# Taking nine chunks of a gated product off VectorE: a ScalarE copy and two GpSimd operations in their place

## The chip, the cores and the metric

The kernel runs on one core of one Trainium2 chip. The metric is the device time of one execution in microseconds (us). The kernel before takes 713.96 us, the median of 3 runs (713.81 to 714.0).

## What is computed

Two things in a row, on x of 4 samples x 12416 tokens x 128 channels. First an attention block with 32 inducing points I: h = mab(I, x), then mab(x, h). Then a gated feed-forward layer of width 1536 on each token. Cut to its core:

```python
def mab(q, kv):                      # softmax attention with one head
    s = scale * (q @ kv.transpose(0, 2, 1))
    a = softmax(s)
    return a @ kv
y = mab(x, mab(I, x))                # (4, 12416, 128)
gate = 1.0 / (1.0 + np.exp(-(y @ w_gate)))
out = (gate * (y @ w_val)) @ w_out   # float32
```

## The kernel before

**Work and blocks.** The tokens of a sample are cut into blocks of 4 x 128 tokens. There are 97 blocks, 24 for each sample and one for the tokens left over. For a block the attention's second half and the two input products of the feed-forward layer are one matmul each: the normalised weights `a2r` (32 per token) times `hwt`, which holds h times the weights. The width of 1536 is 12 *chunks* of 128. A chunk of a block has 512 values in each of the 128 partitions, fp32 in PSUM, which is one bank.

For each chunk the engines do this:

- TensorE fills a bank with the gate's input (`g_ps`) and a bank with the value (`v_ps`), both at L1022 in `hidden_mm`.
- ScalarE takes tanh of half the gate's input from PSUM to fp16 (`t`, L1053, or `xn` at L1045 in the last stretch, where the results go to storage of x that is free by then).
- VectorE makes u = (tanh + 1) * value, from PSUM to fp16, at L1071 in `product`. The factor 0.5 of the sigmoid is left to the end.
- TensorE multiplies u with the chunk's part of w_out: four matmuls of 128 columns, added up over the 12 chunks in one bank, `acc_ps` (L1106 in `project`).
- After the 12th chunk ScalarE moves the bank out, times 0.5 (`o`, L1124), and SyncE stores it.

**The wide stretch.** For blocks 0 to 75 the chunks go in steps of two and one. From block 76 on (step number `T0`; the stretch of the change) no bank is needed for the attention any more, so PSUM is laid out anew: a block has six *steps* of two chunks, called steps 0 to 5 here. `v_ps` is one tile of two banks for a step, and there are two such tiles (tags "vw" and "v2") in turn, so the fill of a step waits until the product of two steps before is through. Three banks (`gw0` to `gw2`) hold gate inputs of single chunks, and one bank is `acc_ps`. VectorE makes one product of 1024 values in each step. ScalarE makes two single tanhs, each in an instruction of its own (`single_gate`).

**The order of the work.** It is written out by hand, and each engine goes through its own queue in order. In the wide stretch a step t is: the fill of v(t), the fills of two gate banks (the second chunk of step t+1 and the first of t+2), the product u(t), the tanh of step t+1's second chunk, then the output matmuls of step t-2's two chunks, one piece of what else is due, and the tanh of step t+2's first chunk. The output matmuls come out of a list of (step, chunk) pairs, `queue`. So the last chunks of a block are multiplied in step 1 of the block behind it, `o` comes there, and the first output matmul of the next block waits for `o`, since `acc_ps` is one bank.

**Other work in the stretch.** The weights `a2r` of the later blocks of the last sample are still made there: ScalarE does an exp (`e`, L662) for four blocks at a time, three times in the stretch (in step 0 of blocks 80, 84 and 89). Behind each GpSimd sums, inverts (L453) and spreads them (`a2n`, L692), and between these it subtracts maxima (L646 to L653).

**Waits.** They are put in from what each instruction reads and writes. Two engines that read the same PSUM tile are also put one behind the other, in the order of the program, unless the kernel says otherwise. It does so in two places, in these lines, of which the first stands at the start of the kernel for two engines that read two banks of a tile:

```python
tc.declare_no_dep(two.ins, one.ins, reason="each reads a bank of its own")
...
tc.declare_no_dep(u.ins, st["tanh"].ins, reason="the gate fill of t + 2 waits for it")
```

Of the kernel before, what the change touches and what calls it, by code (L numbers as in the profile page):

```python
# [9 lines left out]
F32 = mybir.dt.float32  # L10
# [3 lines left out]
ALU = mybir.AluOpType  # L14
# [3 lines left out]
P = 128  # L18
# [8 lines left out]
def kernel(  # L27
# [9 lines left out]
    nc = tc.nc  # L37
    B, N, C = x.shape
    m = inducing.shape[0]
    F = moe_w_gate.shape[1]  # L40
    NJ = F // P
# [19 lines left out]
    op = ctx.enter_context(tc.tile_pool(name="op", bufs=3))  # L61
# [23 lines left out]
    xn, xT = {}, {}  # L85
# [32 lines left out]
    def keep_on(n, tag, src=idle):  # L118
        w_ps = ps.tile([P, 4, P], F32, tag=tag, name="w_ps")
        for _ in range(n):  # L120
            nc.tensor.matmul(w_ps[:], src[:, 0, :], src, start=True, stop=True)
# [11 lines left out]
        out=identf[:],  # L133
        in_=identf[:],
# [662 lines left out]
    for p in range(-2, NS - 3):  # L797
# [13 lines left out]
        if p == EARLY - 2:  # L811
            we = const.tile([P, EARLY], F32, tag="we")
            nc.vector.tensor_reduce(
                out=nml[:, 0:1], in_=nm1[:, 0:EARLY], axis=AX.X, op=ALU.min
            )
            nc.scalar.activation(
                out=we[:], in_=nm1[:, 0:EARLY], func=AF.Exp, bias=nml[:, 0:1], scale=-1.0
# [20 lines left out]
    c0, n = groups[sc]  # L838
# [3 lines left out]
    for j0, tag, copy in ((GC // 2, "v2", nc.scalar.copy), (GC - BC, "g1", nc.vector.tensor_copy)):  # L842
# [26 lines left out]
        out=top[:],  # L869
        in_=mlT_ps.rearrange("o (g r) -> o r g", g=4),  # L870
        axis=AX.X,
        op=ALU.min,
# [5 lines left out]
    for g in range(4):  # L878
# [5 lines left out]
            stop=True,  # L884
# [13 lines left out]
        out=e32l[:], in0=e32[:], scalar1=lsum[:], scalar2=TINY, op0=ALU.mult, op1=ALU.add  # L898
# [5 lines left out]
        out=hw_parts[3],  # L904
        in0=hps[2],
        scalar=wl[:, 3:4],
        in1=hw_parts[2],
# [7 lines left out]
    def h_add(k, first=False, last=False):  # L915
# [15 lines left out]
        out=nmx_a[:], in_=s2_a[:, 0:BC, :], axis=AX.X, op=ALU.max, negate=True  # L931
# [3 lines left out]
        out=low[:],  # L935
        in0=s2_a[:, 0:BC, :],
        in1=nmx_a[:].unsqueeze(2).to_broadcast((P, BC, m)),
        op=ALU.add,
# [4 lines left out]
    for hf, tag in enumerate(("g1", "v1")):  # L943
# [10 lines left out]
        out=a2n_a[:],  # L954
        in0=e_a[:, :, 0:m],
        in1=rs_a.unsqueeze(2).to_broadcast((P, BC, m)),
        op=ALU.mult,
# [19 lines left out]
    def turn_b():  # L977
        rs_b = s2_inverse(nb, sme_b)
        a2n_b = s2_spread(BC, e_b[:, 0:BC, :], rs_b[:, 0:BC], nc.gpsimd)
        s2_turn_dma(0, NLO + BC, BC, a2n_b, "a2second")  # L980
        a2n_c = s2_spread(nb - BC, e_b[:, BC:nb, :], rs_b[:, BC:], nc.gpsimd)
        s2_turn_dma(0, NLO + 2 * BC, nb - BC, a2n_c, "a2r")


    steps = []
# [13 lines left out]
    T0 = first_step[(B - 1, 0)] + 2 * 16  # L999
    assert gates[T0]["j0"] == 0  # L1000
    steps = gates[:T0]
    singles = []
    for i in range(gates[T0]["block"], len(blocks)):
        for j in range(0, NJ, 2):
            steps.append(dict(block=i, j0=j, cnt=2, bank="vw" if j % 4 else "v2"))
        singles += [dict(block=i, j0=j, cnt=1, bank=f"gw{j % 3}") for j in range(NJ)]
    NST = len(steps)

    def hidden_mm(st, what, halves=False):
        tag = st.get("bank") or f"{what}{st['cnt']}"  # L1010
        pt = ps.tile([P, st["cnt"], 512], F32, tag=tag, name=f"{what}_ps")
        pieces, col = [], 0
        for b, c, nb in blocks[st["block"]]:
            pieces += [(k, b, c, nb, col) for k in range(st["cnt"])]
            col += nb * P
        if not halves and st["block"] < len(blocks) - 1:
            pieces.sort(key=lambda p: p[0])
        for k, b, c, nb, col in pieces:
            j = st["j0"] + k
            r = 32 * (j % 2 + (2 if what == "v" else 0))  # L1020
            a2r, o = a2[(b, c)]
            st[what + "end"] = nc.tensor.matmul(  # L1022
                pt[:, k, col : col + nb * P],
                hw[b][r : r + 32, j // 2, :],
                a2r[r : r + 32, o : o + nb, :].rearrange("p j t -> p (j t)"),
                start=True,
                stop=True,
            )
        st[what] = pt

    def gate_fill(t):
        if t < T0 + 2:
            hidden_mm(gates[t], "g", t == 0)

    def ring_t(i, n):
        c = i % 24 * BC
        return xn[B - 2][:, c : c + n * BC, :].rearrange("p (j a) c -> p j (a c)", a=BC)

    def single_fill(i):
        if i < len(singles):  # L1040
            hidden_mm(singles[i], "g")

    def single_gate(i):
        if i < len(singles):
            nc.scalar.activation(out=ring_t(i, 1), in_=singles[i]["g"][:], func=AF.Tanh, scale=0.5)  # L1045

    def gate(t):
        if t < T0 + 2:
# [3 lines left out]
            for c, e in zip(cuts, cuts[1:]):  # L1052
                st["tanh"] = nc.scalar.activation(  # L1053
                    out=st["t"][:, :, c:e], in_=st["g"][:, :, c:e], func=AF.Tanh, scale=0.5
                )

    def product(t):
        st = steps[t]
        hidden_mm(st, "v")
        if t == 0:  # L1060
            keep_on(3, "acc")
        if t < T0:
            gate_fill(t + 2)
        else:
            single_fill(2 * (t - T0) + 3)
            single_fill(2 * (t - T0) + 4)
            st["t"] = ring_t(2 * (t - T0), 2)
        st["u"] = up.tile([P, st["cnt"], 512], F16, tag=f"u{st['cnt']}", name="u16")
        cuts = [0, 256, 512] if t == 0 else [0, 512] if t < NST - 1 else [0, 384, 512]
        for c, e in zip(cuts, cuts[1:]):  # L1070
            u = nc.vector.scalar_tensor_tensor(  # L1071
                out=st["u"][:, :, c:e],
                in0=st["t"][:, :, c:e],
                scalar=1.0,
                in1=st["v"][:, :, c:e],
                op0=ALU.add,
                op1=ALU.mult,
            )
            if t == 0 and c == 0:
                turn_b()  # L1080
        if st["cnt"] == 2 and 4 <= t < T0:

            tc.declare_no_dep(u.ins, st["tanh"].ins, reason="the gate fill of t + 2 waits for it")
            tc.add_manual_dep(
                u.ins, gates[t + 2]["gend"].ins.name, AFTER, reason="tanh, gate fill, product"
            )

    acc = [None]
    queue = [(t, k) for t in range(NST) for k in range(steps[t]["cnt"])]
    queue.reverse()  # L1090

    def project(upto, now, room):
        while queue and queue[-1][0] < upto and room > 0:
            t, k = queue.pop()
            st = steps[t]
            j = st["j0"] + k
            if j == 0:
                acc[0] = ps.tile([P, BC, C], F32, tag="acc", name="acc_ps")
            todo = [(k, i) for i in range(BC)]
            if t == NST - 1:  # L1100
                k, _ = queue.pop()[1], None
                j = st["j0"] + k
                todo = [(n, i) for n in range(2) for i in range(BC - 1)] + [(n, BC - 1) for n in range(2)]
            for n, i in todo:
                e = st["j0"] + n
                nc.tensor.matmul(  # L1106
                    acc[0][:, i, :],
                    st["u"][:, n, ts(i, P)],
                    wo16[:, NI * (e % 2) + e // 2, :],
                    start=(e == 0 and i == 0),  # L1110
                    stop=(e == NJ - 1),
                    skip_group_check=True,
                )
            room -= 1
            if t == NST - 1:
                o32 = op.tile([P, BC, C], F32, tag="o32")
                nc.scalar.mul(out=o32[:, 0:2], in_=acc[0][:, 0:2], mul=0.5)
                nc.scalar.dma_start(ov0[:, 0, 0:2, :], o32[:, 0:2])
                nc.vector.tensor_scalar_mul(out=o32[:, 2:4], in0=acc[0][:, 2:4], scalar1=0.5)
                nc.sync.dma_start(ov0[:, 0, 2:4, :], o32[:, 2:4])  # L1120
            elif j == NJ - 1:
                block = blocks[st["block"]]
                o32 = op.tile([P, BC, C], F32, tag="o32")
                nc.scalar.mul(out=o32[:], in_=acc[0][:], mul=0.5)  # L1124
                b, c, nb = block[0]
                nc.sync.dma_start(ov[b, :, c : c + BC, :], o32[:])
                if now < NST:
                    return True
        return False
# [3 lines left out]
    for b in range(B):  # L1133
# [6 lines left out]
        for s in range(3 if b == 0 else 2, NG - 1):  # L1140
            k = o + 16 * s - 28
# [61 lines left out]
    def beside(slot, late):  # L1203
        for make in plan.pop((slot, late), ()):
            make()

    def waiting(upto):
        n = 0
        for e in reversed(queue):
            if e[0] >= upto:  # L1210
                break
            n += 1
        return n
# [13 lines left out]
    ps.open(ctx, "psw", "vw", "gw0", "gw1", "gw2")  # L1227
    for t in range(T0, NST):
        product(t)
        six, part = divmod(t - T0, 3)  # L1230
        single_gate(2 * (t - T0) + 3)
        for i in range(2):
            if not project(t - 1, t, 1) and waiting(t - 1) >= 2:
                project(t - 1, t, 1)
            if i == 0:
                for slot, late in ([(0, False), (0, True)], [(1, False)], [(1, True)])[part]:
                    beside(T0 // 2 + 2 * six + slot, late)
        single_gate(2 * (t - T0) + 4)
# [32 lines left out]
```

## Time and profile before

| what | value |
|---|---|
| time, median of 3 runs | 713.96 us (713.81 to 714.0) |
| span of the profiled execution | 712.4 us |
| instructions in it | 21620 |
| share of the span busy: TensorE, VectorE, ScalarE, GpSimd | 91%, 97%, 95%, 63% |
| mean granted TensorE clock | 0.998 |
| first and last tanh at L1045 | 565.3 and 705.2 us |
| chain that ended last: VectorE, TensorE, "issue", ScalarE | 38%, 30%, 15%, 14% |

How to read it: one execution was recorded on the chip. Its span goes from the first to the last instruction, and the execution has no time of its own beside that; the median of the runs is 1.6 us above the span, which is what lies around it. In the groups of instructions a row gives line, engine, operation, what is written from what, the shape and the count, then the busy time in us and the mean duration of one in ns, then idle time before it. In the timeline a row gives start and duration in us of instructions merged (xcount), and in brackets how long the engine was idle before and what released it. DVE is VectorE, ACT ScalarE, POOL GpSimd, PE TensorE. Instructions of one engine overlap in the records: the next one starts before the last one's result is written.

### The profile page before, as it was taken

The numbers are of one execution on the slowest core, as the hardware profiler recorded it, in microseconds if no ns is written. First come the engines' busy times: TensorE is split into PE (matmuls) and PEld (weight loads), VectorE is DVE, ScalarE is ACT, GpSimd is POOL, SyncE is SP. The second block draws the span as 40 slices with busy tenths as digits, with TensorE's granted clock in tenths as the row PEclk, the third lists the DMA queues.
The fourth block names the chain that finished last, engine by engine and source line by source line (L and its number), as shares of the span: only waits on it lengthen the run. The fifth ranks groups of instructions, "written<-read, shape, count | busy, mean of one in ns | idle before, by whom it ended". The sixth has DMA issues, their size and how long they took to land.

```text
span 712.4 us, 21620 instructions
## 1 busy us (share of the span) xinstructions
PE 649.5 (91%) x8475; PEld 394.2 (55%) x8475; DVE 694.2 (97%) x806; ACT 678.6 (95%) x1103; POOL 449.2 (63%) x785
## 2 busy tenths in 40 slices
PE   7999899998999999999998989999899999899996
PEld 4555455555555555655555655555555555555555
DVE  4799999999999999999999999999999999999997
ACT  4799999999999999999999999999999999999996
POOL 4568865877558978668657887587748356372300
PEclk9999999999999999999999999999999999999999
DMA  8979964263693174155485142221222131221201
GB/s 171 176 136 174 149 129 103 76 120 81 118 159 81 57 126 103 56 120 114 92 149 112 53 76 67 55 76 38 70 76 61 46 60 60 61 61 46 71 37 46
DMA packets 117110, 65.23 MB, mean 92 GB/s; under 512 B 100208, under 2 KB 101392, under 8 KB 117008
## 3 DMA queue, kind: packets, MB, share of 16 engines
q1 hardware_dynamic: 112320, 49.83, 31.4%
q0 software_dynamic: 4416, 13.90, 11.1%
q8 instruction: 66, 1.08, 0.6%
q14 instruction: 36, 0.29, 0.1%
q10 hardware_dynamic: 272, 0.13, 0.1%
HBM read 27.80 MB, written 25.43 MB: 75 GB/s over the span
## 4 chain that ended last, share of the span: by engine, by line
DVE 38%; PE 30%; issue 15%; ACT 14%; DMA 2%; DVEq 1%; POOL 0%; ACTq 0%; POOLq 0%
DVE u L1071 36%; PE acc_ps L1106 14%; PE v_ps L1022 11%; ACT t L1053 11%; PE g_ps L1022 2%; DMA xn<-in_x_dram 2%; ACT o L1124 2%; ACT xn L1045 1%; PE hp_ps L296 1%; DVE nm L248 1%; DVEq L1071 0%; POOL xn L95 0%; ACT a1T L261 0%; ACT e L662 0%; ACT hwt L483 0%
## 5 line engine op out<-in xcount | busy, mean ns | idle before, releaser
L1071 DVE SCALAR_TENSOR_TENSOR u<-t,v_ps 128x512 f16<-128x512 f16 x609 | 528.8, 947 | 1.0 <-ACT t L1053 0.5
L1053 ACT ACTIVATE t<-g_ps 128x512 f16<-128x512 f32 x609 | 464.5, 821 | 11.0 <-ACT t L1053 4.3
L1106 PE MATMUL acc_ps<-wo,u 128*128 128x128 f16 x4656 | 334.5, 220 | 3.2 <-ACT o L1124 0.8
L1106 PEld LDWEIGHTS <-u 128*128 128x128 f16 x4656 | 262.7, 98 | 112.9 <-issue 109.4
L1022 PE MATMUL v_ps<-a2r,hwt 32*128 32x512 f16 (+1 forms) x1188 | 278.6, 372 | 47.1 <-DVE u L1071 43.5
L1022 PE MATMUL g_ps<-a2r,hwt 32*128 32x512 f16 (+1 forms) x1188 | 293.6, 376 | 0.5 <-DVE u L1071 0.2
L1022 PEld LDWEIGHTS <-hwt 32*128 32x128 f16 x2424 | 92.0, 91 | 156.7 <-issue 104.3
L1071 DVE SCALAR_TENSOR_TENSOR u<-xn,v_ps 128x1024 f16<-128x1024 f16 (+1 forms) x127 | 142.9, 1206 | 0.3 <-PE g_ps L1022 0.3
L1045 ACT ACTIVATE xn<-g_ps 128x512 f16<-128x512 f32 x249 | 129.0, 606 | 1.9 <-PE g_ps L1022 0.6
L692 POOL TENSOR_TENSOR a2n<-e,rs 128x2048 f16<-128x2048 f16 (+3 forms) x25 | 86.8, 3475 | 5.0 <-DVE rs L681 2.1
L670 POOL TENSOR_TENSOR sum<-e 128x256 f32<-128x256 f16 (+1 forms) x23 | 15.4, 672 | 117.0 <-ACT e L662 117.0
L453 POOL TENSOR_TENSOR near<-sme,minus 128x16 f32<-128x16 f32 (+1 forms) x22 | 65.2, 2964 | 1.6
L1124 ACT ACTIVATE o<-acc_ps 128x512 f32<-128x512 f32 x96 | 58.0, 604 | 0.0
L647 POOL TENSOR_SCALAR rise<-rise 128x256 f32<-128x256 f32 (+6 forms) x110 | 30.3, 275 | 9.6
L650 POOL TENSOR_TENSOR top<-top,rise 128x128 f32<-128x128 f32 (+3 forms) x88 | 28.5, 323 | 7.3
L670 POOL TENSOR_TENSOR sum<-sum 128x128 f32<-128x128 f32 (+3 forms) x92 | 28.4, 309 | 7.2
L646 POOL TENSOR_TENSOR rise<-top 128x128 f32<-128x128 f32 (+3 forms) x88 | 27.3, 311 | 6.9
L646 POOL TENSOR_TENSOR rise<-sc 128x256 f32<-128x256 f32 (+1 forms) x18 | 13.3, 736 | 21.2 <-ACT sc L636 21.1
L653 POOL TENSOR_TENSOR sc<-sc,top 128x512 f32<-128x512 f32 (+1 forms) x18 | 19.5, 1086 | 1.4
L602 PEld LDWEIGHTS <-xT 128*128 128x128 f16 x388 | 13.1, 96 | 11.7 <-issue 11.3
L95 POOL DMA_DIRECT2D xn<-in_x_dram x25 | 15.0, 607 | 6.5 <-DMA xn<-in_x_dram 5.6
L602 PE MATMUL s_ps<-hT,xT 128*128 128x32 f16 x388 | 18.1, 178 | 0.1
(161 smaller groups left out, 321.7 us busy)
## 6 DMA issues: line engine op xcount, KB each, us to landing
out_dram<-o SPq DMA_DIRECT2D x96, 256.0 KB, 2.1
xn<-in_x_dram POOLq DMA_DIRECT2D x19, 512.0 KB, 7.2
xn<-in_x_dram POOLq DMA_DIRECT2D x4, 544.0 KB, 6.0
a2r<-a2n SPq DMA_TRANSPOSE x29, 4.4
xT<-xn SPq DMA_TRANSPOSE x27, 4.4
xn<-in_x_dram POOLq DMA_DIRECT2D x1, 384.0 KB, 14.9
wg<-in_moe_w_gate_dram POOLq DMA_DIRECT2D x1, 384.0 KB, 16.4
wv<-in_moe_w_val_dram POOLq DMA_DIRECT2D x1, 384.0 KB, 16.4
```

Of the source, the lines that this page charges most:

```text
L453: nc.gpsimd.tensor_tensor(out=near, in0=x, in1=minus, op=ALU.pow)
L602: nc.tensor.matmul(s2[:, j, :], xT[b][:, c + j, :], hT16[b][:], start=(j == 0), stop=whole and j == j1 - 1, skip_group_check=True,)
L646: nc.gpsimd.tensor_tensor(out=r, in0=far, in1=near, op=ALU.subtract)
L647: nc.gpsimd.tensor_scalar(out=r, in0=r, scalar1=BIG, scalar2=0.0, op0=ALU.min, op1=ALU.max)
L670: nc.gpsimd.tensor_tensor(out=d[:, 0:n, :], in0=src[:, :, 0:w], in1=src[:, :, w : 2 * w], op=ALU.add)
L692: eng.tensor_tensor(out=a2n[:, 0:n, :, :], in0=e.unsqueeze(2).to_broadcast((P, n, 4, m)), in1=rs.unsqueeze(2).unsqueeze(3).to_broadcast((P ...
L1022: st[what + "end"] = nc.tensor.matmul(pt[:, k, col : col + nb * P], hw[b][r : r + 32, j // 2, :], a2r[r : r + 32, o : o + nb, :].rearrange ...
L1045: nc.scalar.activation(out=ring_t(i, 1), in_=singles[i]["g"][:], func=AF.Tanh, scale=0.5)
L1053: st["tanh"] = nc.scalar.activation(out=st["t"][:, :, c:e], in_=st["g"][:, :, c:e], func=AF.Tanh, scale=0.5)
L1071: u = nc.vector.scalar_tensor_tensor(out=st["u"][:, :, c:e], in0=st["t"][:, :, c:e], scalar=1.0, in1=st["v"][:, :, c:e], op0=ALU.add, op1= ...
L1106: nc.tensor.matmul(acc[0][:, i, :], st["u"][:, n, ts(i, P)], wo16[:, NI * (e % 2) + e // 2, :], start=(e == 0 and i == 0), stop=(e == NJ - 1),
L1124: nc.scalar.mul(out=o32[:], in_=acc[0][:], mul=0.5)
```

## The change

In nine blocks of the wide stretch (77, 79, 81, 83, 86, 88, 91, 93 and 95) step 2 is split. VectorE's product at step 2 makes only the first of the two chunks. The second chunk goes another way. ScalarE copies its value from the second bank of `v_ps` to fp32 storage in SBUF (`aside_take`), in storage of x of the last sample, of which four pieces are used in turn. GpSimd multiplies this by the tanh and adds the value itself, which gives the same u = (tanh + 1) * value in fp16 (`aside_product`). The chunk's four output matmuls move from step 4 of the block to the end of the block's list, behind the 12th chunk, which is in step 1 of the next block. So in step 4 four output matmuls are left, and in step 1 of the next block there are twelve. `o` follows the moved chunk.

```diff
+    AWAY = 2
+    aside = {}
+    for i in (5, 7, 9, 11, 14, 16, 19, 21, 23):
+        t = T0 + (i * 4 - 16) * 3 // 2 + AWAY
+        assert steps[t]["j0"] == 2 * AWAY
+        aside[t] = len(aside)
...
+    def aside_take(t):
+        c = aside[t] % 4 * 24
+        spare = xn[B - 1][:, c : c + 24, :].rearrange("p j c -> p (j c)")
+        st = steps[t]
+        st["far"] = spare[:, 0:1024].bitcast(F32)
+        st["mid"] = spare[:, 1024:2048].bitcast(F32)
+        st["u1"] = spare[:, 2048:2560]
+        nc.scalar.copy(out=st["far"], in_=st["v"][:, 1, :])
+
+    def aside_product(t):
+        st = steps[t]
+        nc.gpsimd.tensor_tensor(out=st["mid"], in0=st["far"], in1=st["t"][:, 1, :], op=ALU.mult)
+        nc.gpsimd.tensor_tensor(out=st["u1"], in0=st["mid"], in1=st["far"], op=ALU.add)
...
+        n = 1 if t in aside else st["cnt"]
         for c, e in zip(cuts, cuts[1:]):
             u = nc.vector.scalar_tensor_tensor(
-                out=st["u"][:, :, c:e],
-                in0=st["t"][:, :, c:e],
+                out=st["u"][:, 0:n, c:e],
+                in0=st["t"][:, 0:n, c:e],
                 scalar=1.0,
-                in1=st["v"][:, :, c:e],
+                in1=st["v"][:, 0:n, c:e],
...
+    for t in aside:
+        end = max(k for k in range(NST) if steps[k]["block"] == steps[t]["block"])
+        queue.remove((t, 1))
+        queue.insert(queue.index((end, 1)) + 1, (t, 1))
+    ends = {steps[t]["block"]: (t, k) for t, k in queue}
...
-                    st["u"][:, n, ts(i, P)],
+                    st["u1"][:, ts(i, P)] if t in aside and n else st["u"][:, n, ts(i, P)],
...
-            elif j == NJ - 1:
+            elif ends[st["block"]] == (t, k):
...
         single_gate(2 * (t - T0) + 3)
+        if t in aside:
+            aside_take(t)
+            aside_product(t)
```

**ScalarE at block 81.** In the rows `xn` is the x storage that the tanhs go to (buffer 1758) or the copy goes to (buffer 5420); in brackets stand the engines and DMA queues whose counts the instruction waits for. Before, from the `o` of block 80 on:

```order
L1124 ACTIVATE o_12737<-acc_ps 128x512 [waits DMAHW3_49,PE_49]
L1045 ACTIVATE xn_1758<-g_ps 128x512 [waits DVE_49]
L1045 ACTIVATE xn_1758<-g_ps 128x512 [waits PE_49]
L1045 ACTIVATE xn_1758<-g_ps 128x512 [waits DVE_49,PE_49]
L1045 ACTIVATE xn_1758<-g_ps 128x512 [waits PE_49]
```

And the same place with the change, up to the `o` of block 81:

```order
L1150 ACTIVATE o_13119<-acc_ps 128x512 [waits DMAHW7_49,PE_49]
L1051 ACTIVATE xn_1758<-g_ps 128x512 [waits DVE_49]
L1051 ACTIVATE xn_1758<-g_ps 128x512 [waits PE_49]
L1070 COPY xn_5420<-v_ps 128x512 [waits DMASW1_49,DMASW0_49,DVE_49]
L1051 ACTIVATE xn_1758<-g_ps 128x512 [waits PE_49] x10
L1150 ACTIVATE o_13260<-acc_ps 128x512 [waits DMAHW0_49,PE_49]
```

The copy stands two tanhs behind the `o` of the block before, and ten tanhs wait behind it up to the block's own `o`. It waits for VectorE. In the built program the count that it waits for is that of the half product of its own step: in the first of the nine it waits for 687, while the value fills of that step and of the next one wait for 685 and 686, the products of the two steps before. The same holds for all nine.

**GpSimd at block 81.** `a2n` is the spread weights, `rise` the first of the chain of maxima for later blocks. Before:

```order
L692 TENSOR_TENSOR a2n<-e,rs 128x2048 [waits DMAHW1_49,Pool_49]
L646 TENSOR_TENSOR rise<-xT_3934 128x256
L647 TENSOR_SCALAR rise<-rise 128x256 [waits Pool_49]
L650 TENSOR_TENSOR top<-xT_3934,rise 128x256 [waits Pool_49]
L646 TENSOR_TENSOR rise<-top 128x16x8 [waits Pool_49]
```

With the change:

```order
L1074 TENSOR_TENSOR xn_5420<-xn_5420,xn_1758 128x512 [waits DMASW1_49,Activation_49]
L1075 TENSOR_TENSOR xn_5420<-xn_5420 128x512 [waits DMASW2_49,PE_49,Pool_49]
L646 TENSOR_TENSOR rise<-xT_3934 128x256
L647 TENSOR_SCALAR rise<-rise 128x256 [waits Pool_49]
L650 TENSOR_TENSOR top<-xT_3934,rise 128x256 [waits Pool_49]
```

The two operations of the aside chunk come between the spread and the maxima; the first of them waits for the copy.

More of the change, by code (lines that the diff above doesn't have):

```diff
@@ L1107, in project @@
                     acc[0][:, i, :],
-                    st["u"][:, n, ts(i, P)],
+                    st["u1"][:, ts(i, P)] if t in aside and n else st["u"][:, n, ts(i, P)],
                     wo16[:, NI * (e % 2) + e // 2, :],
                     start=(e == 0 and i == 0),
-                    stop=(e == NJ - 1),
+                    stop=(t == NST - 1 and e == NJ - 1) or ends[st["block"]] == (t, n),
                     skip_group_check=True,
```

## The prediction

> **What bounds the kernel now.** I read the page first, then the wide stretch by windows, then the groups by shape, and last the timeline of block 81 step by step, since in this kernel all engines are busy at once.
>
> ```profile
> span 712.4 us, 21620 instructions
> 571.97:706.60 134.63, 123.35 (x1502) 75.36 (x1499) 134.63 (x120) 132.43 (x260) 49.45 (x82) 1.00 0.21 57
> 594.60 46.47 DVE L1071 SCALAR_TENSOR_TENSOR u<-xn,v_ps 128x1024 f16<-128x1024 f16 x41
> ```
>
> The second row is the stretch from block 77 on. Its columns are TensorE, weight loads, VectorE, ScalarE, GpSimd. VectorE is busy for all of the 134.63 us, with 119 steps of one product each: 1.131 us a step. ScalarE is busy for 132.43 us, so hardly less. The third row, one piece of VectorE's timeline, has 41 products without a gap. So VectorE paces the stretch, and ScalarE is close behind. How close?
>
> ```profile
> 593.77 0.61 ACT L1124 ACTIVATE o<-acc_ps 128x512 f32<-128x512 f32 x1
> 594.25 2.58 ACT L1045 ACTIVATE xn<-g_ps 128x512 f16<-128x512 f32 x5
> 600.30 0.60 ACT L1124 ACTIVATE o<-acc_ps 128x512 f32<-128x512 f32 x1
> 607.03 0.60 ACT L1124 ACTIVATE o<-acc_ps 128x512 f32<-128x512 f32 x1
> ```
>
> With a backlog, five tanhs end 2.45 us after an `o` (596.83 against 594.38), 0.49 each. A block has 12 tanhs and one `o`: 13 x 0.49 = 6.37 us of the 6.79 (6 x 1.131). ScalarE has 0.42 us of slack in a block. VectorE off the bound is worth no more than ScalarE allows.
>
> **Part 1, VectorE: the gain.**
>
> ```profile
> L1071 DVE SCALAR_TENSOR_TENSOR u<-xn,v_ps 128x1024 f16<-128x1024 f16 x125 | 141.7, 1215 | 0.3 <-PE g_ps L1022 0.3
> L1071 DVE SCALAR_TENSOR_TENSOR u<-t,v_ps 128x512 f16<-128x512 f16 x306 | 208.1, 680 | 0.8 <-ACT t L1053 0.5 <-PE g_ps L1022 0.3
> L636 ACT COPY sc<-s_ps 128x512 f32<-128x512 f32 x18 | 10.7, 592 | 0.0
> L375 POOL TENSOR_TENSOR xT<-xT 128x512 f32<-128x512 f32 x7 | 8.9, 1272 | 3.6 <-ACT xT L358 3.5
> ```
>
> A product of 512 takes 0.68 us where one of 1024 takes 1.215, so each aside frees 0.535 us: 9 x 0.535 = 4.8 us at most.
>
> **Part 2, ScalarE: the copy and its wait.** A copy of this shape lasts 0.59 us like a tanh (0.60), so it takes a slot of 0.49. Nine of them are 4.4 us. Two blocks, one of them with a copy, then need 27 x 0.49 = 13.2 us of ScalarE, and VectorE needs 12 x 1.131 - 0.535 = 13.04: by sums alone ScalarE is the bound, and of the 0.535 some 0.34 would be left. But the copy also waits for the half product of its own step, as the order shows, and ten tanhs stand behind it. Block 81 before, where the products of steps 2, 3 and 4 start at 601.39, 602.52 and 603.65:
>
> ```profile
> 601.39 1.21 DVE L1071 SCALAR_TENSOR_TENSOR u<-xn,v_ps 128x1024 f16<-128x1024 f16 x1
> 602.52 2.35 DVE L1071 SCALAR_TENSOR_TENSOR u<-xn,v_ps 128x1024 f16<-128x1024 f16 x2
> 600.80 1.08 ACT L1045 ACTIVATE xn<-g_ps 128x512 f16<-128x512 f32 x2
> 600.80 2.06 ACT L1045 ACTIVATE xn<-g_ps 128x512 f16<-128x512 f32 x4
> 600.39 0.39 PE L1022 MATMUL v_ps<-a2r,hwt 32*128 32x512 f16 x2
> 600.96 0.61 PE L1106 MATMUL acc_ps<-wo,u 128*128 128x128 f16 x8 [0.17 <-ACT o L1124]
> 601.52 0.39 PE L1022 MATMUL v_ps<-a2r,hwt 32*128 32x512 f16 x2
> 604.78 1.22 DVE L1071 SCALAR_TENSOR_TENSOR u<-xn,v_ps 128x1024 f16<-128x1024 f16 x1
> 606.05 0.39 PE L1022 MATMUL v_ps<-a2r,hwt 32*128 32x512 f16 x2 [0.18 <-DVE u L1071]
> ```
>
> The second tanh starts at 601.28 (600.80 + 1.08 - 0.60), so ScalarE is free for the copy at 601.76, and v is in its bank since 600.78. The half product ends at 601.39 + 0.68 = 602.07. From the last two rows a wait across engines takes 0.05 (product ends 606.00, fill starts 606.05), so the copy starts at 602.12: 0.36 us of idle ScalarE. The two tanhs of step 4 then start at 602.61 and 603.10 instead of about 601.76 and 602.23. The second ends at 603.70, and the product of step 4 can start at 603.75. Without any wait the freed VectorE would be there at 603.12, and before it started at 603.65. So **VectorE waits 0.6 us at step 4, and the 0.535 is gone two steps after it was won**, with 0.1 us on top (0.09 by the unrounded starts). All nine copies stand at the same place behind an `o`, so I take 0.09 for each.
>
> **Part 3, the next block's `o`.** After that wait the tanhs have no lead over the products. Before, in block 81's step 4, the second tanh ended at 602.86, 0.79 before the product that reads it. How fast does it come back?
>
> ```profile
> 596.26 0.39 PE L1022 MATMUL v_ps<-a2r,hwt 32*128 32x512 f16 x2
> 597.24 0.39 PE L1022 MATMUL v_ps<-a2r,hwt 32*128 32x512 f16 x2
> 598.23 0.39 PE L1022 MATMUL v_ps<-a2r,hwt 32*128 32x512 f16 x2
> 604.92 0.39 PE L1022 MATMUL g_ps<-a2r,hwt 32*128 32x512 f16 x2
> 605.38 0.60 ACT L1045 ACTIVATE xn<-g_ps 128x512 f16<-128x512 f32 x1
> 607.04 1.22 DVE L1071 SCALAR_TENSOR_TENSOR u<-xn,v_ps 128x1024 f16<-128x1024 f16 x1
> L1106 PE MATMUL acc_ps<-wo,u 128*128 128x128 f16 x4656 | 334.5, 220 | 3.2 <-ACT o L1124 0.8 <-DVE u L1071 0.4
> ```
>
> When TensorE and ScalarE catch up after an exp, a step takes them 0.98 us, so 0.15 of lead a step. Three steps on, at step 1 of the next block, it is 0.45. Before, it was 1.0 there (the second tanh ends at 605.98, and the product that reads it, of block 82's step 1, starts at 607.04). So `o` comes 0.55 later against the products, and the four moved matmuls add up to 4 x 0.056 = 0.22 (eight of 0.22 each took 0.61 in a row, so they start 0.39 / 7 apart). From `o` to a product goes a fixed chain: `o` at 600.30, first output matmul 600.96, fill of step 3's value 601.52, and the product 0.46 later (the time from a fill's start at 604.92 to its reader's at 605.38): 601.98. It started at 602.52, so it had 0.54 of cover. An `o` that is 0.55 to 0.77 later costs 0 to 0.23 at step 3. ScalarE's next two tanhs free gate banks that TensorE fills before it goes on, which costs the like at step 4, and the value fill of step 0 is some 0.05 late for the same reason. Carrying these intervals forward step by step, I get 0.05 at step 0, 0.10 at step 3 and 0.15 at step 4: **0.3 us for each aside**; between 0, if the lead comes back sooner, and 0.5. Behind the asides of blocks 79, 83 and 88 an exp takes a further slot of 0.5 us in step 0, which makes 0.45 of it.
>
> **Part 4, what is hidden.** GpSimd's two operations take 2 x 1.27 = 2.5 us. Block 81 is the tightest, as GpSimd is in a spread there:
>
> ```profile
> 609.71 1.07 POOL L653 TENSOR_TENSOR xT<-xT,top 128x512 f32<-128x512 f32 x1
> 619.45 0.62 ACT L662 ACTIVATE e<-xT 128x512 f16<-128x512 f32 x1
> 599.54 3.61 POOL L692 TENSOR_TENSOR a2n<-e,rs 128x2048 f16<-128x2048 f16 x1
> 598.50:605.30 6.80, 6.41 (x77) 3.71 (x74) 6.80 (x7) 6.80 (x14) 6.22 (x9) 1.00 0.26 70
> ```
>
> The spread ends at 603.15, after the copy (602.72); the two end by 605.8. TensorE wants the chunk behind the 12th one, about 0.7 us into the fill of 606.05: a cover of 1.0 us, and in the other blocks more. Without it TensorE would stop for what is missing. The maxima behind them, which ended at 610.78, end 2.6 us later; the exp that reads them starts at 619.45, 6 us behind that. In the last row VectorE is busy for all 6.80 us with GpSimd busy for 6.22, so neither slows the other. [...] TensorE's matmuls are as many as before; the four taken out of step 4 free nothing, since it waits there for gate banks.
>
> **The sum.** Six asides: 0.09 + 0.3 = 0.39 each, 2.3 us. Three with an exp behind: 0.09 + 0.45 = 0.54 each, 1.6 us. Together +4.0 us: a span of 716.4 and, with the 1.6 us around it, **718.0 us**. With nothing for part 3 it is 9 x 0.09 = 0.8, so 714.8; with 0.5 for six and 0.65 for three it is 5.8, so 719.8.
>
> **The rivals.**
>
> *The lead holds (faster).* If the tanhs were far enough ahead when a copy comes, the stall would end inside that lead. It decides at idle + slot + gain = 0.36 + 0.49 + 0.535 = 1.4 us of lead. Then 4.8 us come off: 709.2. The rows show 0.79 and 1.0, which speaks against it. A weaker form is that the copy does not wait at all: then the second tanh of step 4 ends at 603.34, its product starts at 603.39, 0.26 earlier than before, and with part 3 at 0.3 nothing is left, about 714. [...] The built program has the wait, and no run so far shows the copy without it.) Chance 0.07.
>
> *The stall cancels the gain and nothing follows.* Part 3 is all hidden: 714.8. For it: before, not one of the waits of part 3 shows. Against it: 1.0 us of lead has shrunk to 0.45. Chance 0.16.
>
> *GpSimd is late (slower still).* It decides from 1.8 us for each of the two operations in block 81 (603.15 + 3.6 = 606.75). At twice the 1.27 they would take 5.1 us, and from a copy that ends at 602.7 the chunk would be there at 607.8, 1.05 us late, in each of nine blocks: with the 4.0 of above up to 13 us, 727. Against it, a half-precision input costs GpSimd nothing in these rows:
>
> ```profile
> L646 POOL TENSOR_TENSOR rise<-sc 128x256 f32<-128x256 f32 x15 | 11.0, 730 | 18.2 <-ACT sc L636 18.2
> L670 POOL TENSOR_TENSOR sum<-e 128x256 f32<-128x256 f16 x19 | 12.7, 666 | 92.1 <-ACT e L662 92.1
> ```
>
> Chance 0.04.
>
> **The numbers.** The forecast of 718.0 has 0.73, a tenth of it outside the bounds of part 3. A measurement of this kernel can tell 0.2%, 1.4 us, from no change. Faster by more, below 712.5, has the first rival alone: 0.07. Within 0.2%, up to 715.4, are the second rival and its neighbours: 0.16. Slower, with the last rival: 0.77. The range goes from 714.4, just below the second rival, to 719.8, the upper end of part 3.
>
> **What the next profile would show.** Right: nine products of 512 in the stretch, about 0.68 us; before each copy ScalarE idle for 0.3 to 0.9 us, ended by VectorE's product; VectorE, without gaps before, waiting about 0.6 us for a tanh two steps after each half product, and a further 0.1 to 0.15 us a few times in the next block; no wait of TensorE for GpSimd. Wrong: copies that start right behind the tanh; VectorE without gaps; ScalarE idle less than before; or gaps only at the copies with a time near 715.

## The result and the profile after

The changed kernel takes 718.0 us (median of 4 runs, 717.72 to 719.43), the kernel before 713.98 beside it. The ratio is 1.0057, with a 95% interval of 1.0044 to 1.007: slower by 4.0 us. The forecast was 718.0 (714.4 to 719.8). The ratios of the experiments leave out three executions that lasted 1.9 to 2.7 ms, one of the copy without its wait and two of the kernel before.

The profiled execution is the one of 719.43 us. In it the first product of all starts 1.4 us later than before (31.8 us against 30.4), ahead of anything that the change touches; from there to the last product it is 681.3 us against 677.1, so 4.3 more by the unrounded starts. Behind the start of the last product 4.5 us are left instead of 4.9.

The page's totals of the changed kernel:

```profile
span 717.6 us, 21593 instructions
PE 657.5 (92%) x8475; PEld 390.0 (54%) x8475; DVE 693.2 (97%) x806; ACT 681.5 (95%) x1112; POOL 471.0 (66%) x803
```

VectorE is busy for 1.0 us less than before (694.2) and ScalarE for 2.9 us more, in a longer span. The stretch by windows, from the same product to the same product as before (the first of block 77 to the fifth of block 96), says where the room is now (columns as before: TensorE, weight loads, VectorE, ScalarE, GpSimd, clock):

```profile
573.35:712.25 138.90, 131.22 (x1501) 71.10 (x1499) 133.66 (x120) 135.33 (x269) 71.29 (x100) 1.00 0.20 55
```

Before, VectorE was busy for every hundredth of the stretch. The stretch has grown from 134.63 to 138.90 us, 5.2 of which VectorE is idle, and ScalarE 3.6. The groups of the changed kernel by shape name what it waits for:

```profile
L1092 DVE SCALAR_TENSOR_TENSOR u<-xn,v_ps 128x1024 f16<-128x1024 f16 x116 | 135.5, 1218 | 5.5 <-ACT xn L1051 4.3 <-PE g_ps L1028 0.3
L1092 DVE SCALAR_TENSOR_TENSOR u<-xn,v_ps 128x512 f16<-128x512 f16 x9 | 6.1, 681 | 0.0
L1070 ACT COPY xn<-v_ps 128x512 f32<-128x512 f32 x9 | 5.3, 586 | 1.4 <-DVE u L1092 0.6
L1075 POOL TENSOR_TENSOR xn<-xn 128x512 f16<-128x512 f32 x9 | 11.4, 1271 | 0.7
L1074 POOL TENSOR_TENSOR xn<-xn,xn 128x512 f32<-128x512 f32 x9 | 10.4, 1157 | 48.0 <-ACT xn L1070 48.0
L1150 ACT ACTIVATE o<-acc_ps 128x512 f32<-128x512 f32 x96 | 58.0, 604 | 1.6 <-PE acc_ps L1132 1.5
```

Nine products have shrunk to 0.681 us, as they should. The wide ones had 0.3 us of idle time before them in the whole kernel before, and have 5.5 now, most of it for tanhs. ScalarE idles before the copies, for VectorE, and now also before `o`, for the output matmuls. The page counts an idle time only from the end of a record, and a product's record ends 0.08 us after the next could start (1.215 us long, one each 1.131). By the starts of the products VectorE waits 9.12 us in this stretch of the changed kernel and 0.04 before. 9.12 - 0.04 less the nine times 0.534 that it was freed, 4.81, is +4.27 us, which is all that the stretch has grown by. With 0.4 us less behind the last product that leaves 3.8, against 4.0 between the medians.

Block 81 step by step. ScalarE's timeline of the changed kernel, from the `o` of block 80 to that of block 81:

```profile
602.73 0.60 ACT L1150 ACTIVATE o<-acc_ps 128x512 f32<-128x512 f32 x1
603.22 1.08 ACT L1051 ACTIVATE xn<-g_ps 128x512 f16<-128x512 f32 x2
604.42 0.59 ACT L1070 COPY xn<-v_ps 128x512 f32<-128x512 f32 x1
604.90 5.02 ACT L1051 ACTIVATE xn<-g_ps 128x512 f16<-128x512 f32 x10
610.18 0.60 ACT L1150 ACTIVATE o<-acc_ps 128x512 f32<-128x512 f32 x1 [0.26 <-PE acc_ps L1132]
```

And VectorE's, where the half product of step 2 is the row of 0.68:

```profile
603.70 0.68 DVE L1092 SCALAR_TENSOR_TENSOR u<-xn,v_ps 128x512 f16<-128x512 f16 x1
604.40 1.22 DVE L1092 SCALAR_TENSOR_TENSOR u<-xn,v_ps 128x1024 f16<-128x1024 f16 x1
606.02 1.22 DVE L1092 SCALAR_TENSOR_TENSOR u<-xn,v_ps 128x1024 f16<-128x1024 f16 x1 [0.40 <-ACT xn L1051]
607.16 1.22 DVE L1092 SCALAR_TENSOR_TENSOR u<-xn,v_ps 128x1024 f16<-128x1024 f16 x1
```

Read the two together. The second tanh starts at 603.70 and is through its slot at about 604.19. The copy starts at 604.42, just behind the half product, which ends at 604.38. Two tanhs of 0.49 and 0.60 behind the copy's slot of 0.48 end at 605.98, and the product of step 4 starts at 606.02. From the start of step 2's product to that of step 4's it is 2.32 us. It was 2.26 before (601.39 to 603.65), with a product twice as long in between. Nothing of the 0.535 is left.

GpSimd's timeline there, then TensorE's where it takes the chunk:

```profile
601.97 3.61 POOL L692 TENSOR_TENSOR a2n<-e,rs 128x2048 f16<-128x2048 f16 x1
606.77 1.26 POOL L1075 TENSOR_TENSOR xn<-xn 128x512 f16<-128x512 f32 x1
609.75 0.39 PE L1132 MATMUL acc_ps<-wo,xn 128*128 128x128 f16 x4
```

The chunk is ready at 608.03 and wanted at 609.75: GpSimd is hidden with 1.7 us to spare.

### The profile page after: what moved, and what is told of

The parts are those of the page before. It is cut to its first block, busy times and chain, and to the rows that moved or that the text cites. A ratio compares the mean times of both kernels' runs of the same rounds, so it can differ in the third digit from the quotient of the medians.

```text
span 717.6 us, 21593 instructions
## 1 busy us (share of the span) xinstructions
PE 657.5 (92%) x8475; PEld 390.0 (54%) x8475; DVE 693.2 (97%) x806; ACT 681.5 (95%) x1112; POOL 471.0 (66%) x803
## 4 chain that ended last, share of the span: by engine, by line
DVE 35%; PE 29%; ACT 18%; issue 14%; DMA 2%; DVEq 0%; POOL 0%; ACTq 0%; POOLq 0%
DVE u L1092 34%; PE acc_ps L1132 14%; ACT t L1059 10%; PE v_ps L1028 9%; ACT xn L1051 5%; PE g_ps L1028 3%; DMA xn<-in_x_dram 2%; ACT o L1150 2%; PE hp_ps L296 1%; DVE nm L248 1%; ACT xn L1070 1%; DVEq L1092 0%; POOL xn L95 0%; ACT a1T L261 0%; ACT hwt L483 0%
## 5 line engine op out<-in xcount | busy, mean ns | idle before, releaser
L1028 PE MATMUL g_ps<-a2r,hwt 32*128 32x512 f16 (+1 forms) x1188 | 303.0, 376 | 2.4 <-DVE u L1092 0.2
L1028 PEld LDWEIGHTS <-hwt 32*128 32x128 f16 x2424 | 87.8, 91 | 153.3 <-issue 103.1
L1092 DVE SCALAR_TENSOR_TENSOR u<-xn,v_ps 128x1024 f16<-128x1024 f16 (+2 forms) x127 | 141.9, 1171 | 5.5 <-ACT xn L1051 4.3
L1051 ACT ACTIVATE xn<-g_ps 128x512 f16<-128x512 f32 x249 | 127.0, 611 | 0.7 <-PE g_ps L1028 0.6
L1074 POOL TENSOR_TENSOR xn<-xn,xn 128x512 f32<-128x512 f32 x9 | 10.4, 1157 | 48.0 <-ACT xn L1070 48.0
```

What stands on the lines that cost most here:

```text
L1028: st[what + "end"] = nc.tensor.matmul(pt[:, k, col : col + nb * P], hw[b][r : r + 32, j // 2, :], a2r[r : r + 32, o : o + nb, :].rearrange ...
L1092: u = nc.vector.scalar_tensor_tensor(out=st["u"][:, 0:n, c:e], in0=st["t"][:, 0:n, c:e], scalar=1.0, in1=st["v"][:, 0:n, c:e], op0=ALU.add ...
```

## The experiments

The theory to be tested is the prediction's: ScalarE is nearly full, the copy idles it further by waiting for VectorE's half product, and the freed time goes back two steps later; then the late `o` and the four moved matmuls cost some 0.3 us more in the next block. The rivals: the wait costs nothing, the moved matmuls cost it all, GpSimd is what is late. The kernel before took 714.02, 714.0 and 714.07 us in the three groups of runs.

### The copy without its wait

```diff
-        nc.scalar.copy(out=st["far"], in_=st["v"][:, 1, :])
+        far = nc.scalar.copy(out=st["far"], in_=st["v"][:, 1, :])
+        tc.declare_no_dep(far.ins, st["uend"].ins, reason="each reads a bank of its own")
...
+        st["uend"] = u
```

> The change as it is, but the copy no longer waits for the half product of its own step (the two read two different banks). Theory (the copy's wait costs ScalarE idle time, and then the tanhs have no lead left for the next block's o): the idle time at the copies goes, the wait at step 4 shrinks from 0.49 to about 0.2 us, the waits of the next block stay; 1.4 us slower than before, 715.4 (0.9 to 1.8 slower). Rival 1 (ScalarE's nine further slots cost the time, the idle time is free): no change against the change, 718.0. Rival 2 (the wait is all that is wrong): VectorE's 4.8 us come off, 709 to 710.

> The copy without its wait once more, for its profile alone, since the profiled execution of the first time was a disturbed one. Theory: 715.4; the copies start right behind the tanh before them, and the waits of the products that are left stand at step 4 (0.2 us) and in the next block, at steps 0, 3 and 4. Rival (the wait at step 4 is still about 0.5 us, and something else got shorter): then the idle time was not the cause.

It took 715.43 us, 1.0016 of before (1.0008 to 1.0025). The second expectation is for the same kernel profiled once more (715.47 us), and the views are of that execution. Its groups:

```profile
L1070 ACT COPY xn<-v_ps 128x512 f32<-128x512 f32 x9 | 5.4, 604 | 0.0
L1093 DVE SCALAR_TENSOR_TENSOR u<-xn,v_ps 128x1024 f16<-128x1024 f16 x116 | 135.5, 1218 | 3.2 <-ACT xn L1051 1.9 <-PE g_ps L1028 0.3
L1093 DVE SCALAR_TENSOR_TENSOR u<-xn,v_ps 128x512 f16<-128x512 f16 x9 | 6.1, 681 | 0.0
```

And its timelines around the copy of block 81, ScalarE's and VectorE's:

```profile
602.12 0.60 ACT L1070 COPY xn<-v_ps 128x512 f32<-128x512 f32 x1
```

```profile
601.64 0.68 DVE L1093 SCALAR_TENSOR_TENSOR u<-xn,v_ps 128x512 f16<-128x512 f16 x1
603.74 1.22 DVE L1093 SCALAR_TENSOR_TENSOR u<-xn,v_ps 128x1024 f16<-128x1024 f16 x1 [0.18 <-ACT xn L1051]
```

The copies have no idle time before them, and the copy of block 81 starts while the half product still runs (601.64 to 602.32). The product of step 4 comes 2.10 us behind that of step 2 instead of 2.32. The wait costs 718.0 - 715.43 = 2.6 us, 0.29 for each aside (2.3 us by the starts of the products). But the kernel is still 1.4 us slower than before: with no wait, the copy still takes its slot, and the next block still pays. A half product lasts 0.681 us with the copy beside it, as without, and the copy 0.604 against 0.586. So two reads at the same time, each of a bank of its own, made neither record longer by more than 0.02 us here.

### The copy one tanh later

`aside_take` and `aside_product` are moved behind the tanh that follows, the wait kept:

```diff
-        if t in aside:
-            aside_take(t)
-            aside_product(t)
...
         single_gate(2 * (t - T0) + 4)
+        if t in aside:
+            aside_take(t)
+            aside_product(t)
```

> The wait stays, but the copy and GpSimd's two operations stand at the end of the step, behind the tanh of step t+2's first chunk, so that the half product is through when ScalarE gets there. Theory: no idle time at the copies although they wait for the same product, and the same time as without the wait, 715.4 (0.9 to 1.8 slower than before). Rival (it is the dependency itself, or the copy meeting the product in PSUM, and not ScalarE's idle time): 718. Rival 2 (the slots cost the time): 718 as well.

It took 715.45 us, ratio 1.0021 (1.0012 to 1.0029). Its groups:

```profile
L1070 ACT COPY xn<-v_ps 128x512 f32<-128x512 f32 x9 | 5.6, 617 | 0.0
L1092 DVE SCALAR_TENSOR_TENSOR u<-xn,v_ps 128x1024 f16<-128x1024 f16 x116 | 135.4, 1218 | 3.2 <-ACT xn L1051 1.8 <-PE g_ps L1028 0.3
```

Where the half product is through by the time that the copy's turn comes, the wait is met and costs nothing. The time is the same as with the wait taken out (715.43). Two unlike edits that have only the idle time before the copy in common give the same 2.6 us.

### No copy and nothing on GpSimd

The output matmuls of the nine chunks read old x that lies in the spare storage, so those chunks are left out of the computation; VectorE and the order of the matmuls are as in the change.

```diff
-            aside_take(t)
-            aside_product(t)
+            c = aside[t] % 4 * 24
+            spare = xn[B - 1][:, c : c + 24, :].rearrange("p j c -> p (j c)")
+            steps[t]["u1"] = spare[:, 2048:2560]
```

> The nine chunks' second half of the product is left out altogether: no copy and nothing on GpSimd, and their output matmuls read old x from the storage. What stays of the change is the shorter product and the moved output matmuls. Theory: VectorE's gain is 9 x 0.535 = 4.8 us, but the value fills come too late behind a half product and o comes 0.22 us later, so only about 2.7 us are seen: 711.3 (710.7 to 711.8). Rival (the half products give all of it when nothing is put in their place): 709.2.

It took 711.52 us, ratio 0.9963 (0.995 to 0.9975). Its group of the products, and ScalarE's timeline in block 81:

```profile
L1092 DVE SCALAR_TENSOR_TENSOR u<-xn,v_ps 128x1024 f16<-128x1024 f16 x116 | 133.5, 1215 | 0.9 <-PE g_ps L1028 0.3
```

```profile
599.61 0.60 ACT L1150 ACTIVATE o<-acc_ps 128x512 f32<-128x512 f32 x1
600.10 6.00 ACT L1051 ACTIVATE xn<-g_ps 128x512 f16<-128x512 f32 x12
606.36 0.60 ACT L1150 ACTIVATE o<-acc_ps 128x512 f32<-128x512 f32 x1 [0.26 <-PE acc_ps L1132]
```

With the chunk made by nobody, the gain is 2.5 us of the 4.8. VectorE still waits behind each half product, by the product starts 0.16 us at step 4 (0.08 in blocks 86 and 91) and up to 0.10 at step 3, and ScalarE has 12 tanhs in one piece and then waits 0.26 us for the moved matmuls. So the most that this order of work could give is 2.5 us, and the copies have to come out of that.

### The whole product kept

The copy, its wait and GpSimd stay, and VectorE makes both chunks as before (the second result is unused).

```diff
-        n = 1 if t in aside else st["cnt"]
+        n = st["cnt"]
```

> VectorE makes both chunks in the nine steps as before, and the copy, GpSimd's operations and the moved matmuls stay: the change's costs without its gain. Theory: the copy waits for a product of 1.215 instead of 0.68 us, so ScalarE idles 0.9 us at each; 9.0 us slower than before, 723.0 (8.5 to 9.5). Rival 1 (only slots count): ScalarE has 0.42 us of slack in a block and 0.85 in two, a slot takes 0.49, so nothing to 1 us slower, 714 to 715; or, if the 4.0 of the change and the 4.8 of its gain just add up, 8.8, which this run cannot tell from the theory by the time, but by ScalarE's idle time before the copies.

It took 730.13 us (726.37 to 734.76), ratio 1.023 (1.0199 to 1.0261): a miss of 7 us. The windows of its profiled execution (727.66 us; the columns as above, the clock third from the end):

```profile
574.00:578.00 4.00, 3.42 (x27) 1.15 (x24) 3.49 (x4) 3.35 (x7) 2.13 (x2) 0.98 1.19 150
578.00:581.00 3.00, 3.00 (x25) 1.76 (x24) 2.23 (x2) 2.24 (x5) 2.66 (x6) 0.50 0.31 68
583.00:590.00 7.00, 6.74 (x82) 3.74 (x80) 6.88 (x7) 7.00 (x15) 2.41 (x7) 1.00 0.10 37
```

And a pair of fills in TensorE's timeline within the middle window, which takes 0.39 us elsewhere:

```profile
579.16 0.61 PE L1028 MATMUL v_ps<-a2r,hwt 32*128 32x512 f16 x2
```

The granted clock falls to half four times in the stretch, for 3.41 us each (from 577.83, 608.55, 646.10 and 683.64), behind the asides of blocks 77, 81, 86 and 91, and VectorE then waits up to 0.85 us a step. Away from these places it waits 0.91 us for an aside (0.59 at step 4, then 0.07, 0.08 and 0.16 in the next block), and 1.06 where an exp stands behind. Six and three of these come to 8.6 us, an estimate near the 9.0 that were forecast. ScalarE's idle time before the copies, by which the theory was to be told from costs that just add up, is in its group of the copies:

```profile
L1070 ACT COPY xn<-v_ps 128x512 f32<-128x512 f32 x9 | 5.3, 585 | 6.2 <-DVE u L1092 6.2
```

It is 0.68 us each by the records and 0.77 to 0.93 by the slots, where 0.9 was expected, so the wait is what grew. The rest of the 16 us goes with the falls of TensorE's clock, which no step of the theory had. In the profiled execution of the change the clock stays at full in the stretch.

### No wait, and the whole product

Without the wait, VectorE's product is made as long as before; it reads the first bank twice, so that it does not meet the copy in the second, and its second result is unused.

```diff
-                out=st["u"][:, 0:n, c:e],
-                in0=st["t"][:, 0:n, c:e],
+                out=st["u"][:, :, c:e],
+                in0=st["t"][:, :, c:e],
...
-                in1=st["v"][:, 0:n, c:e],
+                in1=st["v"][:, 0:1, c:e].to_broadcast((P, 2, e - c)) if t in aside else st["v"][:, :, c:e],
```

> The copy has no wait, and VectorE's product in the nine steps is as long as before the change, but reads only the first of the two banks, twice; the second result is not used. So VectorE gains nothing and ScalarE, GpSimd and the moved matmuls do what they do in the run without the wait. Theory: without the wait ScalarE and the chain through o are the bound in these blocks, so the shorter product is worth nothing: 715.4, as with it (0.9 to 1.8 slower than before), and TensorE's granted clock stays at full speed. Rival (the costs and VectorE's 4.8 us just add up): 1.4 + 4.8 slower, 720.2.

It took 715.51 us, ratio 1.0017 (1.0008 to 1.0025). Its group of products:

```profile
L1093 DVE SCALAR_TENSOR_TENSOR u<-xn,v_ps 128x1024 f16<-128x1024 f16 x125 | 142.8, 1215 | 1.1 <-PE g_ps L1028 0.3 <-issue 0.2
```

Against 715.43 with the short product: 4.8 us less work on VectorE is worth nothing there. The bound beside the asides is ScalarE and the chain through `o`. VectorE's load no longer sets the time, and only its idle time differs (3.2 us against 1.1).

### The chunk's matmuls sooner, and fewer asides

First the wait out, and the chunk put behind step t + 2 in the list of output matmuls, so that it is no longer the last of its block:

```diff
-        end = max(k for k in range(NST) if steps[k]["block"] == steps[t]["block"])
+        end = t + 2
```

> The copy without its wait, and the moved chunk's four output matmuls come behind the chunks of step 4 instead of behind the block's last chunk, so that o is not behind them. Theory (o comes too late in the next block, by the four matmuls and by the lost lead): the waits at steps 0, 3 and 4 of the next block shrink, 0.7 us slower than before, 714.7 (0 to 1.1 slower). Rival (the four matmuls cost nothing, only the lead counts): as without the wait, 715.4.

It took 714.85 us, ratio 1.0012 (1.0003 to 1.0022). Its group of `o`:

```profile
L1152 ACT ACTIVATE o<-acc_ps 128x512 f32<-128x512 f32 x96 | 58.1, 605 | 0.0
```

The 1.6 us before `o` are gone, and 0.6 us of the time. Then the same with six blocks, those without an exp behind (77, 81, 86, 91, 93, 95), the aside in step 1 and its matmuls behind step t + 3:

```diff
-    AWAY = 2
+    AWAY = 1
...
-    for i in (5, 7, 9, 11, 14, 16, 19, 21, 23):
+    for i in (5, 9, 14, 19, 21, 23):
...
-        end = max(k for k in range(NST) if steps[k]["block"] == steps[t]["block"])
+        end = t + 3
```

> Only the six blocks with no exp behind, the aside in step 1 instead of step 2, no wait at the copy, and the moved matmuls behind the chunks of step 4. Theory: with the copy off the slots of the exp, no idle time and o on time, a little is left of the 6 x 0.535 = 3.2 us: 0.7 us faster than before, 713.3 (0.4 to 0.9 faster). Rival 1 (ScalarE's slots are the bound, whatever their place): 714 to 715. Rival 2 (nothing but idle time and the moved matmuls was wrong): 710.8.

It took 713.32 us, ratio 0.9992 (0.9983 to 1.0001). That is 4.7 us below the change and 0.7 below before; the interval does not tell it from before. Its group of products:

```profile
L1093 DVE SCALAR_TENSOR_TENSOR u<-xn,v_ps 128x1024 f16<-128x1024 f16 x119 | 136.2, 1216 | 2.3 <-PE g_ps L1028 2.2
```

What is left of the waits is now for TensorE's gate fills instead of for tanhs.

### The change in six blocks

Only the list of blocks is cut to those six; the wait, the step and the order are the change's.

> The change as it is, but only in the six blocks with no exp behind them. Theory: 6 x 0.42 = 2.5 us slower than before, 716.5 (2.2 to 2.8), so that the three blocks with an exp behind cost 0.5 each. Rival (the exps make most of the loss): 714.5 or less.

It took 716.09 us, ratio 1.0029 (1.0018 to 1.004): 2.0 us slower than before, 0.34 for each aside, somewhat under the expected bounds. The other three, with an exp behind, would then cost 718.0 - 716.1 = 1.9, or 0.64 each, though the interval of 0.8 us to either side leaves this split rough. The product starts of the change's own trace split it better: part 3 below.

### A third operation on GpSimd

```diff
+        nc.gpsimd.tensor_tensor(out=st["u1"], in0=st["mid"], in1=st["far"], op=ALU.add)
```

> The change with GpSimd's second operation made twice, so that a chunk takes GpSimd 1.35 us longer. Theory (GpSimd is covered): 718.0, as the change; in block 81 its last operation then ends 0.3 us before TensorE wants the chunk. Rival (TensorE or VectorE pays for GpSimd's work): up to 9 x 1.35 = 12 us more, and already a tenth of that, 719.2, would speak for it.

It took 718.31 us, ratio 1.0061 (1.0048 to 1.0074), the change's own within the interval. Three of its six executions took 717.65 to 717.75 us, where the change's fastest took 717.72. In the profiled one (718.86 us) TensorE's clock fell once, behind the aside of block 95, where VectorE's waits of the next block come to 1.6 us instead of 0.4:

```profile
703.52:706.93 3.41, 3.41 (x53) 2.63 (x54) 2.51 (x3) 2.36 (x6) 1.44 (x2) 0.50 0.00 0
```

Whether the third operation has a part in that is not shown. In block 81, GpSimd's timeline and TensorE's:

```profile
606.40 1.27 POOL L1076 TENSOR_TENSOR xn<-xn 128x512 f16<-128x512 f32 x1
```

```profile
608.03 0.39 PE L1133 MATMUL acc_ps<-wo,xn 128*128 128x128 f16 x4
```

Half as much work again ends at 607.67, still 0.36 us before it is wanted. GpSimd is off the path.

## Why the prediction was right

**Part 1, the gain.** The half products take 0.681 us for the 0.680 forecast. That not all of the 4.8 us could be kept is shown by the run without copies: 2.5 at most in this order of work.

**Part 2, the copy's wait.** Forecast: 0.36 us of idle ScalarE in block 81, a wait of 0.6 at step 4, a net cost of 0.09. Measured: 0.23 of idle, waits of 0.49 at step 4 and 0.10 at step 3, which the forecast did not have, a net 0.06. The mechanism is shown three ways: the wait taken out (715.43), the wait met (715.45), and no copy (711.52). The idle time was oversized because the forecast took ScalarE to be as far ahead as before, while in the run it already came later: the second tanh of step 3 starts with the half product (603.70), where before it started 0.11 ahead of it (601.28 against 601.39). In blocks 86 and 91, three blocks behind the aside before them instead of two, ScalarE is ahead again:

```profile
639.30 0.59 ACT L1070 COPY xn<-v_ps 128x512 f32<-128x512 f32 x1 [0.28 <-DVE u L1092]
640.90 1.22 DVE L1092 SCALAR_TENSOR_TENSOR u<-xn,v_ps 128x1024 f16<-128x1024 f16 x1 [0.48 <-ACT xn L1051]
```

The copy's idle time is 0.40 us by the slots there, and the waits are 0.57 at step 4 and 0.02 at step 3: the same sum. What counts is the fixed chain half product, copy, two tanhs, product: 2.32 us in all nine, whatever the lead.

**Part 3, the next block's `o`.** Forecast: 0.05, 0.10 and 0.15 at steps 0, 3 and 4 of the next block, 0.3 for each aside. Measured by the product starts: 0.07, 0.09 and 0.16, together 0.32. VectorE's timeline of the changed kernel in block 82 (steps 3 and 4):

```profile
611.85 1.22 DVE L1092 SCALAR_TENSOR_TENSOR u<-xn,v_ps 128x1024 f16<-128x1024 f16 x1
613.14 1.22 DVE L1092 SCALAR_TENSOR_TENSOR u<-xn,v_ps 128x1024 f16<-128x1024 f16 x1
```

1.29 us lie between them where 1.131 would do. TensorE's timeline shows the cause in the first matmul behind the late `o`:

```profile
610.83 0.38 PE L1132 MATMUL acc_ps<-wo,u 128*128 128x128 f16 x4 [0.36 <-ACT o L1150]
```

With the exps of blocks 80, 84 and 89 it is 0.47 to 0.49 (forecast 0.45), and 0.10 more in block 90. With part 2 an aside costs 0.38 us in five of the six blocks without an exp, 0.50 in block 95, and 0.53 to 0.65 in the other three, where the forecast had 0.39 and 0.54. The moved matmuls alone account for 0.6 us of part 3 (715.43 against 714.85). The forecast put the rest down to the lead that the tanhs lose by the copy's wait. The run without the wait shows 0.07, 0.08 and 0.16 in block 82 all the same: without the wait, the copy's slot beside the shorter product and the moved matmuls are enough to bring these waits, and the wait adds nothing to them.

**Part 4, GpSimd.** Forecast: 2.5 us hidden with a cover of 1.0. Measured: 1.16 + 1.27 = 2.43 with 1.7 to spare; the third operation confirms it. VectorE's products do not grow beside it: in the stretch of the changed kernel the 18 of 1024 values that GpSimd is busy beside nearly from start to end last 1.218 us in the mean, the 34 with GpSimd idle 1.217.

**The sum** of +4.0 is what was measured, but its terms are not. Part 2 cost 9 x 0.06 = 0.5 us where the forecast had 0.8, part 3 cost 4.27 - 0.53 = 3.7 where it had 3.15, and 0.4 us came off behind the last product, which it did not have. The mechanism holds; that the total was met to a tenth of a us is luck, since these misses cancel.

**The rivals.** "The lead holds" falls: even with the copies gone the time is 711.5, not 709.2. Its weaker form, no wait, was given about 714 and came to 715.4. Step 4's product then comes 0.16 us sooner than before in block 81 (2.10 against 2.26), not 0.26, and the next block still costs 0.32 to 0.59. That the shorter product is worth nothing beside this is shown by the run with no wait and the whole product. "Nothing follows" (714.8) falls by the waits in the next block. "GpSimd is late" falls by the third operation.

What stays open: why TensorE's clock falls. With the whole product kept, TensorE is never idle for over 0.5 us in the stretch, and in the 3.41 us ahead of each fall it is busy for 2.71 to 2.87. Ahead of the fall with the third operation it is busy for 3.24. The kernel before has a stretch as long with 2.79 (the first sum of the row), at full clock:

```profile
692.57:695.98 3.41, 2.79 (x37) 1.87 (x35) 3.41 (x4) 3.32 (x7) 0.00 (x0) 1.00 0.00 0
```

And TensorE idles for 0.77 us ahead of the fill at 89.45 in the kernel before, with the granted clock at 1.00 from 86 to 93. So neither the idle times nor the busy share ahead of a fall decide by themselves here.

## What to carry to other kernels

Work moved off a saturated engine is worth at most the slack of the engine that takes it: compare both in the stretch (134.6 and 132.4 of 134.6 us before the change), with the time that an instruction costs in a backlog (0.49 us), not its record (0.60). Before an instruction goes into a nearly full queue that is worked in order, look at what it waits for and at what stands behind it; a wait of 0.23 us there, in block 81, stands for the 0.29 that each aside lost, and moving the same copy back by one tanh took 2.6 us off. An order between two reads of one tile may be put in without need, and where the two read banks of their own it can be declared away: for the copy and the half product that took 2.6 us off here (715.43 against 718.0), and neither record grew by more than 0.02 us.

## What was not expected of the hardware

With the whole product kept, the granted clock of TensorE fell to 0.50 for 3.41 us at a time, in an execution with no idle time of TensorE over 0.5 us in that stretch, and the time went from the forecast 723 to 726 to 735 us. The falls start 30.72, 37.55 and 37.54 us apart, which is nine, eleven and eleven times 3.41. Within the first of them a pair of fills took 0.61 us, for 0.39 elsewhere. An idle time of over 0.5 us is not what brought these falls; what did is not shown.
